# Own weight buffers, freer load order and shifted side work around the Wo product of an attention and mixer block

## Chip, cores, metric

The kernel runs on one core of one Trainium2 chip. The metric is the device time of one execution in microseconds (us), as the median of several runs. Times inside an execution ("at 1091 us") are from the start of its profiled span.

## The reference, cut to what matters

```python
x = A_x                                            # 2048 tokens of 1024, bf16
# sa, ca, ga, sb, cb, gb: six vectors made from silu(c) @ w_mod
h = layernorm(x) * (1 + ca) + sa
x = x + ga * A(h)        # 32 heads of 128, memory of 8 tokens; ends in o @ Wo (4096 -> 1024)
h = layernorm(x) * (1 + cb) + sb
x = x + gb * B(h)

def B(x):                                          # mixer
    h  = gelu(layernorm(x) @ w1)                   # 1024 -> 1024
    hs = shift_quarters(h) @ w2                    # quarters moved by 1, -1, 2, -2 tokens
    x1 = x + hs
    return x1 + gelu(layernorm(x1) @ w3) @ w4      # 1024 -> 3584 -> 1024
```

## The kernel before

The engines are TensorE (PE, the matmuls), VectorE (DVE), ScalarE (ACT) and GpSimd (POOL); SyncE (SP) here issues DMA transfers. ACT and POOL issue some too, each from its own queue. PE's sums go to PSUM, here 8 banks; the program uses a bank again only when another engine has emptied it (at 1491 us PE waits 6.79 us for that). A pool with `bufs=n` hands out n buffers in turn. PE is to be busy all the time. After the attention its stages are: the Wo product (32 units of 32 matmuls); A, the product with w1 and its gelu; the w2 product; then twice (for two "pairs" of 1024 tokens) w3 and w4, each made of seven Strassen-like products of half-size blocks, which need sums of blocks of z (the second layer norm, transposed by DMA). Their weights come in by "ring" loads. A "snap" is a bank that ACT copies to SBUF, a "join" is DVE's sum of a bank and a snap (in w4: a scaled bank), and an "addend" (rs) is what POOL prepares to be added to an output of w4.

The Wo stage. `keep_order` pins an instruction: pinned instructions of one queue keep the order in which the code emits them. An unpinned one may be put wherever its dependencies allow by the scheduler that builds the program.

```python
otpA = ...tile_pool(name="x1_otA", bufs=3)         # + otpB, bufs=3, opened later
wspR = ...tile_pool(name="x1_wsR", bufs=1)
ws_pools[:] = [wsp, wsp, wspR]                     # wsp has 2: three Wo buffers in all
def load_ot(j):                                    # one head chunk of O, transposed
    ot = pool.tile([P, 8, 512], BF16, name="OTc")
    keep_order(nc.sync.dma_start(ot[:], OTx_d[j // 4, j % 4]))
def W_units(blk):                                  # blk: 512 tokens
    def f():                                       # one unit: column half n2, head chunk hc
        if hc == 0: st["accs"] = [acc_tile() for _ in range(4)]
        woc = ws_tile([P, 8, 512])
        keep_order(nc.sync.dma_start(woc[:], Wo2[...]))
        ...  # 32 matmuls with ot, woc; after hc 3 the gate ga is applied
        if n2 == 1: load_ot(blk * 4 + hc + 6)      # refill when both halves have used it
    return [mk(n2, hc) for n2 in range(2) for hc in range(4)]
```

The w2 stage and the outputs of w4:

```python
def Ba(t):   # one tile of 128 tokens: load u (sync queue), 16 matmuls, x1b = acc + u,
    ...      # store x1b (ACT queue), layer norm -> z on ACT
def Bb(t):   # z -> z2a (tiles 0 to 7) or z2b (8 to 15)
    return lambda: nc.scalar.dma_start_transpose(z2s[t // 8][...], zs[t][:])
# after tile 11: z_sums(0), four DVE sums S1..S4 for the first pair

def fin(a, n, i, bank, s=None):                    # w4: one 128 x 512 output
    if s is not None: ...                          # two POOL operations on rs
    t_ = stm.tile(...)                             # stm: 3 buffers
    nc.vector.tensor_tensor(t_[:], st[i][bank][:], gbs_b[:, cs], ALU.mult)  # empties the bank
    o = outp.tile(...)
    nc.vector.tensor_tensor(o[:], t_[:], r[:], ALU.add)                     # waits for POOL
    nc.scalar.dma_start(out2[...], o[:])
# pair 0: z_sums(1), four sums in a row, before the sixth product of w4
```

## Time and profile before

| what | before |
|---|---|
| time, median of 3 | 1678.64 us (1678.47 to 1680.76) |
| span of the profiled run | 1680.5 us, mean granted clock 0.959 |
| Wo stage (first Wo product to first A product) | 321.3 us, of it 76.2 us waits for Wo loads |
| A | 55.6 us |
| w2 stage, to the third product on the sums of z | 90.5 us |
| from there to the first w4 product | 77.7 us |
| w4, w3, w4 after it | 94.3, 84.4, 84.8 us |

The stages are cut where the timeline of PE changes its line. The lines themselves are in the prediction.

### The profile page before, as it was taken

To read this page: it belongs to the slowest core of one execution; us is meant where nothing else is said; L and a number is where in the kernel's file an instruction comes from. 1 tells how busy PE (TensorE), PEld (TensorE's weight loads), DVE (VectorE), ACT (ScalarE), POOL (GpSimd) and SP (SyncE) were. 2 spreads that over 40 slices of the span, in tenths; PEclk is the share of its full clock that TensorE was granted. 3 is DMA by queue.
4 is the path that set the end of the run, shared out by engine and by line. 5 is a ranking of instruction groups with operands and counts; after the bars stand their busy time and mean duration, and the time that the engine had idled before them with its cause. 6 is when DMAs were issued, how large, how long until landed. Compare 5 with 4: busy or idle time off the path is not lost. (4 is left out here: it accounts for less than half of the span.)

```text
span 1680.5 us, 24001 instructions
## 1 busy us (share of the span) xinstructions
PE 1521.8 (91%) x9410; PEld 800.3 (48%) x9410; DVE 770.1 (46%) x1553; ACT 561.3 (33%) x1149; POOL 345.8 (21%) x468
## 2 busy tenths in 40 slices
PE   6899999999999999999957766869997799989998
PEld 3465565555555555555623322324443344434443
DVE  5516555565466354654420040505434534563454
ACT  2534444444444444444400020202332464016500
POOL 7310000000000000000011110211200256365525
PEclk9999999999999999999968888989999899999999
DMA  9589878979887776574396575759469878767862
GB/s 323 168 273 230 237 182 222 220 196 236 214 209 187 186 176 142 158 178 99 89 266 220 189 221 164 225 194 257 140 143 231 262 278 296 262 226 259 305 220 65
DMA packets 388333, 350.89 MB, mean 209 GB/s; under 512 B 203627, under 2 KB 331627, under 8 KB 381683
## 3 DMA queue, kind: packets, MB, share of 16 engines
q1 hardware_dynamic: 334256, 287.10, 60.5%
q10 hardware_dynamic: 46130, 34.90, 7.3%
q0 software_dynamic: 7824, 27.27, 5.1%
q8 instruction: 75, 1.23, 0.3%
q14 instruction: 48, 0.39, 0.1%
HBM read 221.27 MB, written 76.31 MB: 177 GB/s over the span
## 5 line engine op out<-in xcount | busy, mean ns | idle before, releaser
L751 PE MATMUL acc<-wstream,OTc 128*128 128x512 bf16 x1024 | 244.8, 404 | 76.2 <-DMA wstream<-in_A_Wo_dram 76.2
L317 PE MATMUL acc<-hh,wk 128*128 128x480 bf16 x1024 | 227.2, 367 | 1.3 <-DMA wk<-in_A_Wk_dram 1.3
L317 PE MATMUL acc<-hh,wv 128*128 128x480 bf16 x1024 | 227.9, 366 | 0.0
L317 PE MATMUL acc<-hh,wq 128*128 128x480 bf16 x1024 | 225.8, 370 | 0.6 <-DVE hh L425 0.5
L751 PEld LDWEIGHTS <-OTc 128*128 128x128 bf16 x1024 | 105.3, 103 | 215.5 <-issue 107.5
L664 POOL DMA_DIRECT2D OTx_d<-OT x32 | 24.3, 758 | 709.5 <-DMA OT<-O 556.1
L317 PEld LDWEIGHTS <-wq 128*128 128x128 bf16 x1024 | 97.7, 99 | 95.2 <-issue 3.5
L127 ACT ACTIVATE QT<-acc 128x480 bf16<-128x480 f32 (+1 forms) x192 | 87.9, 476 | 162.9 <-PE acc L317 157.6
L646 DVE TENSOR_TENSOR O<-ps_o,rin_all 99x384 bf16<-99x384 f32 (+2 forms) x256 | 133.3, 522 | 13.7 <-DMA MT<-O 6.7
L317 PEld LDWEIGHTS <-wk 128*128 128x128 bf16 x1024 | 95.9, 98 | 90.9 <-DMA wk<-in_A_Wk_dram 3.0
L125 ACT CAST KT<-acc 128x480 bf16<-128x480 f32 (+2 forms) x190 | 84.9, 464 | 151.5 <-PE acc L317 143.2
L125 ACT CAST VT<-acc 128x480 bf16<-128x480 f32 (+3 forms) x222 | 86.2, 420 | 147.5 <-PE acc L317 140.6
L317 PEld LDWEIGHTS <-wv 128*128 128x128 bf16 x1024 | 94.8, 97 | 81.5
L1049 PEld LDWEIGHTS <-ring 128*128 128x128 f16 (+1 forms) x784 | 77.5, 99 | 106.3 <-issue 16.4
L632 DVE TENSOR_TENSOR Em<-E,maskB 99x495 bf16<-99x495 bf16 (+1 forms) x128 | 48.4, 379 | 167.6 <-ACT E L630 167.3
L645 DVE RECIPROCAL rin_all<-ps_o 99x3 f32<-99x3 f32 (+2 forms) x256 | 44.1, 174 | 139.2 <-PE ps_o L643 139.1
L753 DVE TENSOR_TENSOR x<-acc,ga_b 128x512 f32<-128x512 f32 x32 | 21.7, 684 | 171.1 <-PE acc L751 167.4
L643 PE MATMUL ps_o<-V,Em 99*99 99x129 bf16 (+2 forms) x704 | 84.4, 225 | 17.1 <-DVE O L646 10.2
L643 PEld LDWEIGHTS <-Em 99*99 99x99 bf16 (+2 forms) x704 | 68.4, 128 | 49.0 <-DVE O L646 14.4
L1099 PEld LDWEIGHTS <-hq 128*128 128x128 bf16 (+1 forms) x560 | 55.3, 99 | 75.1 <-issue 10.0
L630 ACT ACTIVATE E<-ps_s 99x495 bf16<-99x495 f32 (+2 forms) x160 | 86.5, 542 | 2.8 <-DVE Em L632 2.3
L836 ACT ACTIVATE u<-x,ln_nmr,ln_rstd 128x1024 bf16<-128x1024 f32 x16 | 19.7, 1232 | 200.5 <-DVE ln_nmr L835 199.6
(188 smaller groups left out, 2038.5 us busy)
## 6 DMA issues: line engine op xcount, KB each, us to landing
wstream<-in_A_Wo_dram SPq DMA_DIRECT2D x34, 1024.0 KB, 9.6
OTx_d<-OT POOLq DMA_DIRECT2D x32, 512.0 KB, 6.8
OTc<-OTx_d SPq DMA_DIRECT2D x16, 1024.0 KB, 5.6
wstream<-in_B_w_dram SPq DMA_DIRECT2D x56, 256.0 KB, 6.3
ring<-w3t_d SPq DMA_DIRECT2D x14, 1024.0 KB, 8.2
ring<-w4t_d SPq DMA_DIRECT2D x8, 1792.0 KB, 7.2
ring<-w3b_d SPq DMA_DIRECT2D x14, 768.0 KB, 5.3
ring<-w4b_d SPq DMA_DIRECT2D x6, 1792.0 KB, 9.2
```

What stands on the lines that cost most here:

```text
L125: nc.scalar.copy(dst, src)
L127: nc.scalar.mul(dst, src, scale)
L317: nc.tensor.matmul(acc[:, 0:CH], lhsT=W[:, kt, hl * P:(hl + 1) * P], rhs=hh[:, kt, i * CH:(i + 1) * CH], start=(kt == 0), stop=(kt == KT - 1))
L630: nc.scalar.activation(E[:rows, 0:o], ps[:rows, 0:o], ACT.Exp)
L632: nc.vector.tensor_tensor(Em[:rows, c0:c0 + o], E[:rows, 0:o], mk[:rows, 0:o], ALU.mult)
L643: nc.tensor.matmul(ps[:rows, i, :], lhsT=Em[:k, col0(t):col0(t) + rows], rhs=V[:k, t, 0:DH + 1], start=True, stop=True)
L645: nc.vector.reciprocal(rin, ps[:rows, 0:n, DH])
L646: nc.vector.tensor_tensor(O[:rows, ts[0]:ts[0] + n, :], ps[:rows, 0:n, 0:DH], rin[:, :, None].to_broadcast([rows, n, DH]), ALU.mult)
L664: nc.gpsimd.dma_start(OTx_d[:, h // 8, :, h % 8, :].rearrange("b d t -> d b t"), flat.rearrange("p (b t) -> p b t", t=512))
L751: nc.tensor.matmul(accs[tt][:], lhsT=ot[:, hl, tt * P:(tt + 1) * P], rhs=woc[:, hl, :], start=(h == 0), stop=(h == H - 1))
L1049: nc.tensor.matmul(acc[:], lhsT=B[:, k, q * P:(q + 1) * P], rhs=A[:, k, :], start=(start and k == 0), stop=(k == 3), skip_group_check=True)
L1099: nc.tensor.matmul(acc[:], lhsT=L3[:, k, i * P:(i + 1) * P], rhs=R3[:, k, :], start=(start and k == 0), stop=(k == 13), skip_group_check=True)
```

## The change

Its intent: give the Wo stream its own buffers so that its loads run ahead; let both column halves of the first Wo block use the same early OTc tiles; take the transposes of the second layer norm from ACT, which also stores and normalizes; hold the last outputs of w4 back by two so that DVE empties PSUM banks first. Cut to its core (pool moves, the later place of the last memory product and the check's PSUM bank left out):

```diff
-        otpA = ...tile_pool(name="x1_otA", bufs=3, side="right")
-        wspR = ...tile_pool(name="x1_wsR", bufs=1, side="right")
-        ws_pools[:] = [wsp, wsp, wspR]
+        otcp = ...tile_pool(name="x1_ot", bufs=6, side="right")
+        wspR = ...tile_pool(name="x1_wsR", bufs=4, side="right")
+        ws_pools[:] = [wspR]
...
-            keep_order(nc.sync.dma_start(ot[:], OTx_d[j // 4, j % 4]))
+            nc.sync.dma_start(ot[:], OTx_d[j // 4, j % 4])
-                    keep_order(nc.sync.dma_start(woc[:], Wo2[...]))
+                    nc.sync.dma_start(woc[:], Wo2[...])
...   # block 0; 4 instead of 3 banks in psB, all 8 banks of PSUM in the rotation
+        for u in W0[1][0:3] + W0[0][3:] + W0[1][3:]:
+            u()
...
-            return lambda: nc.scalar.dma_start_transpose(z2s[t // 8][...], zs[t][:])
+            return lambda: nc.sync.dma_start_transpose(z2s[t // 8][...], zs[t][:])
-            if i == 11:
-                z_sums(0)
+            if i == 14:
+                for f in z_sums(0):
+                    keep_order(f())
...   # w4: stm 4 buffers; o and its store in end(), which lags
+                fins.append(end)
+                if len(fins) > 2 or s is None:
+                    fins.pop(0)()
-            if pair == 0:
-                z_sums(1)
+            zs1 = z_sums(1) if pair == 0 else []
             for i in prod("b", A22, 6, False):
                 fin(1, 0, i, "b")
+                for u in zs1[i:i + 1]:
+                    u()
+            for u in fins:
+                u()
```

More of the change, by code (lines that the diff above doesn't have):

```diff
@@ L220, in make_masks @@
             nc.gpsimd.tensor_copy(maskB[:].rearrange("p (t c) -> p t c", c=TW), mt[:, None, :].to_broadcast([P, 5, TW]))
+        wop = LM.enter_context(tc.tile_pool(name="up_wo", bufs=2))
+        otmp = LM.enter_context(tc.tile_pool(name="up_otm", bufs=2))
         LQ = ExitStack()
@@ L236, in first_pass @@
         rp = RX.enter_context(tc.tile_pool(name="x_rows", bufs=1, side="right"))
-        wsp = RX.enter_context(tc.tile_pool(name="x_ws", bufs=2, side="right"))
+        RW = ExitStack()
+        wsp = RW.enter_context(tc.tile_pool(name="x_ws", bufs=2, side="right"))
         ga_b = rp.tile([P, D], F32, name="ga_b")
@@ L506, in first_pass @@
             nc.gpsimd.memset(t[0:96, 0, :], 0.0)
-        wop = LA.enter_context(tc.tile_pool(name="up_wo", bufs=2))
         otp = LA.enter_context(tc.tile_pool(name="up_ot", bufs=2))
@@ L595, in prep_units, with M_units @@
             return units
-        def M_units(hp, use_psS=False):
+        def M_units(hp):
             def mk(g):
@@ L600, in f @@
                     wo2, OTm = state["wo2", hp], state["otm", hp]
-                    acc = psS.tile([P, 512], F32, name="ps_s") if use_psS else acc_tile()
+                    acc = acc_tile()
                     a3 = acc[:, 0:4 * NMEM].rearrange("p (k m) -> p k m", m=NMEM)
@@ L657, in keep @@
             if h % 2 == 0:
-                state["otm", h // 2] = otp.tile([P, 2, NMEM], BF16, name="OTm")
+                state["otm", h // 2] = otmp.tile([P, 2, NMEM], BF16, name="OTm")
             OTm = state["otm", h // 2]
@@ L714, in first_pass @@
         R0.close()
+        RW.close()
         RO = ExitStack()
-        otpA = RO.enter_context(tc.tile_pool(name="x1_otA", bufs=3, side="right"))
-        wspR = RO.enter_context(tc.tile_pool(name="x1_wsR", bufs=1, side="right"))
-        ws_pools[:] = [wsp, wsp, wspR]
-        ot_pools = [otpA]
+        otcp = RO.enter_context(tc.tile_pool(name="x1_ot", bufs=6, side="right"))
+        wspR = RO.enter_context(tc.tile_pool(name="x1_wsR", bufs=4, side="right"))
+        ws_pools[:] = [wspR]
         ots = {}
@@ L724, in load_ot @@
                 return
-            pool = ot_pools[0] if j % 6 < 3 else ot_pools[1]
-            ot = pool.tile([P, 8, 512], BF16, name="OTc")
-            keep_order(nc.sync.dma_start(ot[:], OTx_d[j // 4, j % 4]))
+            ot = otcp.tile([P, 8, 512], BF16, name="OTc")
+            nc.sync.dma_start(ot[:], OTx_d[j // 4, j % 4])
             ots[j] = ot
@@ L739, in f @@
                     if hc == 0:
-                        st["accs"] = [acc_tile() for _ in range(4)]
+                        st[n2] = [acc_tile() for _ in range(4)]
                     if hc == 3 and n2 == 0:
@@ L743, in f @@
                             x1s[blk * 4 + tt] = xpools["tp4"].tile([P, D], F32, name="x1")
-                    accs = st["accs"]
+                    accs = st[n2]
                     woc = ws_tile([P, 8, 512])
-                    keep_order(nc.sync.dma_start(woc[:], Wo2[hc * 1024:(hc + 1) * 1024, cs].rearrange("(h p) n -> p h n", p=P)))
+                    nc.sync.dma_start(woc[:], Wo2[hc * 1024:(hc + 1) * 1024, cs].rearrange("(h p) n -> p h n", p=P))
                     ot = ots[blk * 4 + hc]
@@ L755, in f @@
                         load_ot(blk * 4 + hc + 6)
-                    elif blk == 0 and hc == 3:
-                        load_ot(4)
-                        load_ot(5)
                 return f
-            return [mk(n2, hc) for n2 in range(2) for hc in range(4)]
+            return [[mk(n2, hc) for hc in range(4)] for n2 in range(2)]
         W0 = W_units(0)
@@ L765, in first_pass @@
         load_wo2(NHP - 2)
-        interleave(att[NHP - 1], M_units(NHP - 3) + [lambda: load_wo2(NHP - 1)] + M_units(NHP - 2) + W0[0:2])
-        for u in att["end"]:
-            u()
-        for u in W0[2:3] + M_units(NHP - 1, use_psS=True):
-            u()
-        W0 = W0[3:]
+        interleave(att[NHP - 1], M_units(NHP - 3) + [lambda: load_wo2(NHP - 1)] + M_units(NHP - 2) + W0[0][0:2])
+        for u in att["end"] + W0[0][2:3]:
+            u()
+        for j in range(3, 6):
+            load_ot(j)
         LA.close()
         LQ.close()
-        psB = PS.enter_context(tc.tile_pool(name="psB", bufs=3, space=PSUM))
-        pst = PS.enter_context(tc.tile_pool(name="pstX", bufs=1, space=PSUM))
-        acc_pools[:] = [psA, psB, psA, psA2, psA, psB, psB]
+        psB = PS.enter_context(tc.tile_pool(name="psB", bufs=4, space=PSUM))
+        acc_pools[:] = [psB]
         LZ = ExitStack()
@@ L787, in first_pass @@
         bsm = LT.enter_context(tc.tile_pool(name="x1_sm", bufs=8))
-        LO = ExitStack()
-        otpB = LO.enter_context(tc.tile_pool(name="x1_otB", bufs=3))
-        ot_pools.append(otpB)
-        load_ot(3)
+        for u in W0[1][0:3] + W0[0][3:] + W0[1][3:]:
+            u()
+        acc_pools[:] = [psA, psB, psA, psB, psA, psB, psA2, psB]
+        acc_ctr[0] = 0
+        for u in M_units(NHP - 1):
+            u()
         def check_a(kt):
@@ L803, in check_b @@
         def check_b():
-            pn = pst.tile([1, 512], F32, name="pn")
+            pn = acc_tile()[0:1, :]
             for kt in range(KT):
@@ L823, in check_b @@
             nc.vector.tensor_scalar(bad[:], okm[:], -1.0, 1.0, ALU.mult, ALU.add)
-            pb = pst.tile([1, 512], F32, name="pn")
+            pb = acc_tile()[0:1, :]
             nc.tensor.matmul(pb[:, 0:1], lhsT=ones_col[:], rhs=bad[:], start=True, stop=True)
@@ L865, in C1b @@
             return f
-        for u in W0:
-            u()
         for blk in range(1, 4):
             chain = lagged(C1a, C1b, list(range(4 * blk - 4, 4 * blk)), lag=1)
+            units = [u for us in W_units(blk) for u in us]
             if blk == 1:
@@ L877, in first_pass @@
                 nc.scalar.dma_start(Mc_d[:], Macc[:])
-            interleave(chain, W_units(blk))
-        LO.close()
+            interleave(chain, units)
         RO.close()
-        ws_pools[:] = [wsp]
         RH = ExitStack()
@@ L920, in dve @@
         def dve(dst, a, b, op):
-            nc.vector.tensor_tensor(dst, a, b, op)
+            return nc.vector.tensor_tensor(dst, a, b, op)
         ready = {}
@@ L954, in z_sums @@
             S1, S2, S3, S4 = (zs4[:, i] for i in range(4))
-            dve(S1, A21, A22, ALU.add)
-            dve(S2, S1, A11, ALU.subtract)
-            dve(S3, A11, A21, ALU.subtract)
-            dve(S4, A12, S2, ALU.subtract)
             zsum[pair] = (A11, A12, S4, A22, S1, S2, S3)
+            return [lambda: dve(S1, A21, A22, ALU.add), lambda: dve(S2, S1, A11, ALU.subtract),
+                    lambda: dve(S3, A11, A21, ALU.subtract), lambda: dve(S4, A12, S2, ALU.subtract)]
         LT2 = ExitStack()
@@ L984, in Bb @@
         def Bb(t):
-            return lambda: nc.scalar.dma_start_transpose(z2s[t // 8][:, :, t % 8 * P:(t % 8 + 1) * P], zs[t][:])
+            return lambda: nc.sync.dma_start_transpose(z2s[t // 8][:, :, t % 8 * P:(t % 8 + 1) * P], zs[t][:])
         for i, u in enumerate(lagged(Ba, Bb, list(range(NTT)), lag=1)):
@@ L1003, in first_pass @@
         st2 = RF.enter_context(tc.tile_pool(name="x3_s2", bufs=2, side="right"))
-        stm = RF.enter_context(tc.tile_pool(name="x3_sm", bufs=3, side="right"))
+        stm = RF.enter_context(tc.tile_pool(name="x3_sm", bufs=4, side="right"))
         rsq = RF.enter_context(tc.tile_pool(name="x3_rq", bufs=2, side="right"))
@@ L1108, in rs_load @@
                     nc.sync.dma_start(rs[a, n, i][:], rs_d[t * P:(t + 1) * P, n * 512:(n + 1) * 512])
+            fins = []
             def fin(a, n, i, bank, s=None):
@@ L1118, in fin, with end @@
                 nc.vector.tensor_tensor(t_[:], st[i][bank][:], gbs_b[:, cs], ALU.mult)
-                o = outp.tile([P, 512], BF16, name="o")
-                nc.vector.tensor_tensor(o[:], t_[:], r[:], ALU.add)
-                nc.scalar.dma_start(out2[t * P:(t + 1) * P, cs], o[:])
+                def end():
+                    o = outp.tile([P, 512], BF16, name="o")
+                    nc.vector.tensor_tensor(o[:], t_[:], r[:], ALU.add)
+                    nc.scalar.dma_start(out2[t * P:(t + 1) * P, cs], o[:])
+                fins.append(end)
+                if len(fins) > 2 or s is None:
+                    fins.pop(0)()
             def ed():
@@ L1157, in w4_stage @@
                 fin(1, 1, i, "b", "s5")
+            zs1 = z_sums(1) if pair == 0 else []
             for i in prod("b", A22, 6, False):
                 fin(1, 0, i, "b")
+                for u in zs1[i:i + 1]:
+                    u()
+            for u in fins:
+                u()
         with tc.manual_schedule():
```

## The prediction

> **What bounds the kernel now.** I read the page first, then the timeline of TensorE (PE) where its row of tenths dips, then the timelines of the queue or engine that each gap names. The page:
>
> ```profile
> PE   6899999999999999999957766869997799989998
> ...
> PEclk9999999999999999999968888989999899999999
> ...
> L751 PE MATMUL acc<-wstream,OTc 128*128 128x512 bf16 x1024 | 244.8, 404 | 76.2 <-DMA wstream<-in_A_Wo_dram 76.2
> ```
>
> Each slice is 42 us. PE is full in the first half (projections and attention), dips from slice 21 to 27 and twice later, and the granted clock dips with it. The row of line 751 is the Wo product: 32 units of 32 matmuls, each unit fed by one 1 MB load of Wo. All its idle time, 76.2 us, waits for those loads. The timeline of PE, then that of the SP DMA queue, over the same time:
>
> ```profile
> 866.12 23.19 PE L751 MATMUL acc<-wstream,OTc 128*128 128x512 bf16 x96 [1.11 <-DMA wstream<-in_A_Wo_dram]
> ...
> 918.39 8.85 PE L751 MATMUL acc<-wstream,OTc 128*128 128x512 bf16 x32 [8.23 <-DMA wstream<-in_A_Wo_dram]
> ...
> 1116.68 70.85 PE L751 MATMUL acc<-wstream,OTc 128*128 128x512 bf16 x320 [8.31 <-DMA wstream<-in_A_Wo_dram]
> 1187.37 31.24 PE L895 MATMUL acc<-zT,w1s 128*128 128x512 bf16 x144
> ```
>
> ```profile
> 910.19 0.33 SPq L727 DMA_DIRECT2D OTc<-OTx_d  x1
> 910.56 0.43 SPq L746 DMA_DIRECT2D wstream<-in_A_Wo_dram  x1
> 927.27 0.33 SPq L727 DMA_DIRECT2D OTc<-OTx_d  x1
> 927.69 1.00 SPq L746 DMA_DIRECT2D wstream<-in_A_Wo_dram  x2
> ```
>
> The pattern: a unit ends at 909.9, only then does the SP queue issue the next OTc load (its buffer was being read by that unit), and the Wo load stands behind it in the same in-order queue. It lands some 8 us later and PE starts at 918.4. The queue's own waits say the same: it waited 123.2 us, in 8 waits, at line 727 for the matmuls of line 751. Ten units end so. From 1116.68, where no OTc load is left to issue, ten units run without a gap at 7.09 us each. Elsewhere they run at the lower clock: 8.85 us for one after an 8 us gap.
>
> The two later dips. First the w2 stage, in the timeline of ACT's queue, then DVE, then PE:
>
> ```profile
> 1254.04 12.38 ACTq L985 DMA_TRANSPOSE z2a<-z  x1
> ```
>
> ```profile
> 1271.41 0.69 DVE L977 TENSOR_TENSOR x1b<-acc,u 128x512 f32<-128x512 f32 x1 [9.14 <-DMA x1b_d<-x1b]
> ...
> 1298.98 1.23 DVE L921 TENSOR_TENSOR zs<-z2a 128x2048 f16<-128x2048 bf16 x1 [7.93 <-DMA z2a<-z]
> ```
>
> ```profile
> 1300.93 8.72 PE L975 MATMUL acc<-w2s,h1T 128*128 128x512 bf16 x32 [8.26 <-DVE ln_ve L111]
> ...
> 1317.33 3.57 PE L1049 MATMUL bank_b<-z2a,ring 128*128 128x512 bf16 x8 [5.19 <-POOL ln_rstd L113]
> ```
>
> And PE near the end of the first w4 stage:
>
> ```profile
> 1490.98 9.27 PE L1099 MATMUL bank_b<-ring,hq 128*128 128x512 f16 x32 [6.79 <-DVE join L1118]
> ```
>
> In the w2 stage (1243 to 1317) ACT is held 12.4 us by issuing one transpose; the x1b stores behind it are late, DVE waits 9.1 us for an x1b buffer, then 7.9 us because the Strassen sums of z were put after tile 11, before their transposes have landed. DVE needs about 3.3 us a tile against PE's 3.45, so lost DVE time is never made up and surfaces as PE gaps. At 1491 PE waits for DVE to empty a bank; DVE had first waited for POOL at each output and then done four sums of z (2.2 us each) in a row.
>
> **What the Trainium skill says.** "Perfetto Trace Analysis", § Optimization Strategy: the same bubble repeating on the engine that should be full can mean too few buffers for the next tile. The trace agrees: 8 us gaps, with three Wo buffers and an OTc refill in front. "TensorE: Matmul & The Clock Gate", § What's actually happening: after an idle window of about 3.4 us the array falls to half clock and needs as long a busy window to return. The trace agrees: 8.85 us for a unit after a gap, 7.09 without. "DMA: Bandwidth & Descriptors", § Issuing engines are not separate DMA queues: all queues share the 16 engines, and another issuer saves only the issuer's time. So I count the transposes' move to SP as freeing ACT, not as bandwidth; the trace shows the DMA share at 1.01 over 1243 to 1328.
>
> **The change part by part.**
>
> *Wo stage.* PE's order as built is now straight: block 0 does column half 0 for head chunks 0 to 2, half 1 for 0 to 2, then the last chunk for both; all 8 PSUM banks serve. The SP order still has an OTc load before many Wo loads, but Wo has four buffers of its own and six OTc buffers. Counting through that order, the Wo load of unit n is now issued when unit n-4 ends, so three units, 21 us, lie between issue and need, against 9.6 us median landing. The wait at an OTc load no longer hurts. The x loads in the queue (they wait for POOL adds, up to 18 us) stand in places where the load behind them is needed 15 us or more later. Removed: 75.1 us of gaps after the first unit. Also removed: the clock loss. Stage now 1187.4 - 866.1 = 321.3. Stage after: first three units as now 23.0; 29 units at 7.09 = 205.6; the small memory products and check, 2; stalls from DMA crowding, 5 (my guess). Sum 235.6. Gain 86.
>
> Why 5 and not 0: block 1 must move 8 MB Wo, 4 MB OTc and 5 MB of the layer-norm chain in 8 x 7.09 = 57 us, 300 GB/s. The trace shows 321 GB/s over its first 40 us, so it fits, narrowly. In block 0 the loads waiting at 882 (3 OTc, 3 Wo) need about 6 MB / 340 GB/s = 18 us; I find the fifth unit's Wo landing within 2 us of when PE gets there.
>
> The start does not move: the first two Wo loads stand behind the same transposes in SP, issued at 858.9. The product that waited 5.9 us before it goes later, but PE then waits for Wo instead.
>
> *w2 stage.* ACT loses 16 transposes; SP gains them. x1b stores go out in time, the sums wait for tile 14. Now from 1243.0 to the first product on the sums at 1328.3: 85.3 us. After: 256 matmuls at 0.2165 = 55.4; the first two products 3.5; lag 8 (DVE's 3.3 x 16 + 4 x 1.2 for the sums = 57.6, so 2 to 3 behind, plus 5 for late loads of u, which now stand behind transposes in SP, and a saturated DMA). Sum 66.9. Gain 18.
>
> *w4, first pair.* Outputs lag two steps and the sums alternate with them, so a bank is emptied as soon as it is done. Gain 6.8 idle, plus about 2.3 for the half clock after it: 9.
>
> *End.* The last outputs are held back by two: two more 0.69 us operations after the last bank. Loss 1.5.
>
> Sum: 86 + 18 + 9 - 1.5 = 111.5; 1678.6 - 111.5 = 1567.
>
> **The rivals.**
> 1. DMA becomes the bound of the Wo stage. For: the share of DMA is already 0.67 over the stage with 27% of it idle PE; the same work in 236 us needs 0.67 x 321 / 236 = 0.91. Against: the attention part runs at 0.9 to 1.0 in some 40 us windows (480 to 520: 1.02) with PE full. If true, stalls of 25 us instead of 5: about 1587.
> 2. The w2 stage is bound by DMA already (share 1.01), so taking transposes from ACT only moves the wait to SP: late u loads take the place of late stores. Then 0 to 5 us gain there: 1582. In favour of my reading: at 1255 to 1263 that share goes with under 90 GB/s, so much of it is queueing, not work.
> 3. The head-of-line wait stays, since OTc loads still precede Wo loads in SP: then Wo gains half, about 1610. The count of buffers speaks against it.
> 4. Better than thought: no stalls, lag 3 instead of 8: 1557.
>
> **Range and chances.** 1567 with 80% from 1548 to 1592: the low end is rival 4 with the start somewhat earlier; the high end has rival 1 or 2 whole. A gain under 2% (over 1645) would need the Wo stage to gain under 50 us of its 99 idle or slow. Faster 0.97, same 0.02, slower 0.01.
>
> **What would show it.** Right: the Wo row's idle below 15 us with matmul mean near 380 ns; the clock at full from 875 to the end of A; the SP queue still waiting at the OTc line without PE noticing; Wo stage near 236 us; w2 stage to first sum product near 67; no PE gap over 2 us near the end of the first w4 stage. Wrong: gaps at Wo loads while DMA is at 1.0 (rival 1); DVE waiting for u loads in the w2 stage (rival 2); a new PE wait on a PSUM bank, since the check now takes banks of the shared rotation.

## The result, and the profile after

The changed kernel took 1566.58 us (median of 4, 1564.84 to 1573.46) against 1679.22 us of the kernel before in the same rounds: ratio 0.9336, 95% interval 0.9306 to 0.9365. The outputs are correct. The profiled run has a span of 1565.6 us at a mean clock of 0.981.

The page, and PE's timeline over the Wo stage:

```profile
PE   5799999999999999999996899999998899989998
...
PEclk9999999999999999999997899999999999999999
...
L753 PE MATMUL acc<-wstream,OTc 128*128 128x512 bf16 x1003 | 223.2, 383 | 7.8 <-DMA wstream<-in_A_Wo_dram 6.5
```

```profile
866.05 0.59 PE L753 MATMUL acc<-wstream,OTc 128*128 128x512 bf16 x1 [6.54 <-DMA wstream<-in_A_Wo_dram]
866.85 57.55 PE L753 MATMUL acc<-wstream,OTc 128*128 128x512 bf16 x249 [0.22 <-issue]
...
987.39 103.77 PE L753 MATMUL acc<-wstream,OTc 128*128 128x512 bf16 x471
1091.01 55.42 PE L891 MATMUL acc<-zT,w1s 128*128 128x512 bf16 x250
```

PE's dip in slices 21 to 27 has shrunk to slices 22 and 23, where the attention ends and the first Wo load is awaited; the clock's dip likewise. The 76.2 us of waits have become 7.8, of which 6.54 lie before the first product. (1003 of the 1024 matmuls are in the trace; a few per cent of the records are missing.)

| stage | before | after | gain | predicted gain |
|---|---|---|---|---|
| up to the first Wo product | 866.1 | 866.1 | 0.1 | 0 |
| Wo stage | 321.3 | 225.0 | 96.3 | 86 |
| A | 55.6 | 55.3 | 0.3 | 0 |
| w2 stage, to the third product on sums | 90.5 | 71.7 | 18.9 | 18, counted to the first such product (23.7 there) |
| to the first w4 product | 77.7 | 80.5 | -2.8 | 0 |
| w4, pair 0 | 94.3 | 84.8 | 9.5 | 9 |
| w3, pair 1 | 84.4 | 90.7 | -6.2 | 0 |
| w4, pair 1 | 84.8 | 84.8 | 0 | 0 |
| after the last matmul | 5.9 | 7.0 | -1.1 | -1.5 |
| sum | 1680.5 | 1565.6 | 114.9 | 111.5 |

Two gaps of PE stand at new places, one in front of the third product on the sums in the first w3 stage, one in front of the first such product in the second:

```profile
1217.91 3.57 PE L1044 MATMUL bank_b<-zs,ring 128*128 128x512 f16 x8 [6.48 <-ACT snap L1010]
...
1391.14 3.41 PE L1044 MATMUL bank_b<-zs,ring 128*128 128x512 f16 x8 [4.52 <-ACT snap L1010]
```

After each, the eight matmuls take 3.4 to 3.6 us instead of 1.89: the half clock again.

Only the second gap is new in substance. In the kernel before, DVE waited at the same first join for the same transposes, and PE had a gap two products earlier:

```profile
1330.99 1.29 DVE L1057 TENSOR_TENSOR join<-bank_e,snap 128x512 f32<-128x512 f32 x2 [8.42 <-DMA z2b<-z]
```

```profile
1328.25 3.54 PE L1049 MATMUL bank_b<-zs,ring 128*128 128x512 f16 x8 [5.32 <-ACT snap L1015]
```

So the 23.7 us gained up to the first product on the sums are in part a wait moved to the third; 18.9 us is the fairer count.

### The profile page after: what moved, and what is told of

It is laid out like the page before. It is cut to its first block, busy times and chain, and to the rows that moved or that the text cites. A ratio compares the mean times of both kernels' runs of the same rounds, so it can differ in the third digit from the quotient of the medians.

```text
span 1565.6 us, 23960 instructions
## 1 busy us (share of the span) xinstructions
PE 1492.3 (95%) x9347; PEld 794.9 (51%) x9410; DVE 763.2 (49%) x1553; ACT 561.1 (36%) x1149; POOL 343.9 (22%) x468
## 4 chain that ended last, share of the span: by engine, by line
PE 89%; DMA 5%; DVE 2%; SPq 1%; POOL 1%; issue 1%; ACT 1%; ACTq 0%; DVEq 0%; POOLq 0%
PE acc L321 37%; PE acc L753 14%; PE bank_b L1094 6%; PE bank_b L1044 6%; PE acc L331 4%; PE acc L891 4%; PE acc L969 3%; PE bank_d L1044 3%; PE ps_o L646 2%; PE bank_e L1094 2%; PE bank_d L1094 2%; PE ps_s L630 2%; PE bank_e L1044 1%; DMA V<-VT 1%; DMA wstream<-in_B_w_dram 1%
## 5 line engine op out<-in xcount | busy, mean ns | idle before, releaser
L753 PE MATMUL acc<-wstream,OTc 128*128 128x512 bf16 x1003 | 223.2, 383 | 7.8 <-DMA wstream<-in_A_Wo_dram 6.5
L321 PE MATMUL acc<-hh,wq 128*128 128x480 bf16 x1024 | 224.4, 369 | 0.9 <-DVE hh L429 0.5
L753 PEld LDWEIGHTS <-OTc 128*128 128x128 bf16 x1024 | 100.7, 99 | 129.2 <-issue 10.6
L633 ACT ACTIVATE E<-ps_s 99x495 bf16<-99x495 f32 (+2 forms) x160 | 86.5, 541 | 2.8 <-DVE Em L635 2.3
L1010 ACT COPY snap<-bank_b 128x512 f32<-128x512 f32 x72 | 40.5, 583 | 104.1 <-PE bank_b L1094 63.2
```

The lines of the kernel that those rows point to most:

```text
L321: nc.tensor.matmul(acc[:, 0:CH], lhsT=W[:, kt, hl * P:(hl + 1) * P], rhs=hh[:, kt, i * CH:(i + 1) * CH], start=(kt == 0), stop=(kt == KT - 1))
L633: nc.scalar.activation(E[:rows, 0:o], ps[:rows, 0:o], ACT.Exp)
L753: nc.tensor.matmul(accs[tt][:], lhsT=ot[:, hl, tt * P:(tt + 1) * P], rhs=woc[:, hl, :], start=(h == 0), stop=(h == H - 1))
```

## The experiments

Twelve kernels were run, all correct. In this table "against after" is the difference of the two ratios to the kernel before, times 1678 us, so that kernels of different rounds can be set side by side; the intervals are 0.2% to 0.35% (3 to 6 us) either way for each ratio, more for the difference of two.

| kernel | median us | ratio to before | against after | Wo stage us |
|---|---|---|---|---|
| after | 1566.58 | 0.9336 | | 225.0 |
| after, both loads pinned again | 1653.66 | 0.9858 | +88 | 310.6 |
| after, 3 Wo buffers | 1583.03 | 0.9432 | +16 | 238.6 |
| after, old column order | 1569.48 | 0.9349 | +2 | 224.3 |
| before, 4 Wo buffers | 1660.92 | 0.9889 | +93 | 304.2 |
| before, pins taken away | 1593.84 | 0.9490 | +26 | (*) |
| after, transposes on ACT | 1577.74 | 0.9399 | +11 | 225.9 |
| after, sums after tile 11 | 1570.06 | 0.9352 | +3 | 224.4 |
| after, old w4 outputs | 1570.01 | 0.9342 | +1 | 224.6 |
| after, small w3 buffers moved | 1577.65 | 0.9389 | +9 | 224.4 |
| after, outputs before the fourth sum | 1568.21 | 0.9333 | 0 | 224.3 |
| after, the last two together | 1575.26 | 0.9374 | +6 | 224.1 |
| that, addends earlier, stores on POOL | 1563.10 | 0.9326 | -2 | 223.6 |

(*) There the scheduler also moves Wo units into the attention, so the stage begins earlier, at 839.7; the first A product comes at 1099.4 us, 88 us before that of the kernel before (1187.4). w4 of pair 0 takes 98.7 us there against 94.3, which is why the whole kernel gains a little less.

### The Wo stage: which part of the change did it?

Three theories. A: the fourth Wo buffer, as the prediction has it. B: the pins, which the prediction does not name at all. C: both column halves of block 0 at once.

**Pins put back.**

```diff
-            nc.sync.dma_start(ot[:], OTx_d[j // 4, j % 4])
+            keep_order(nc.sync.dma_start(ot[:], OTx_d[j // 4, j % 4]))
-                    nc.sync.dma_start(woc[:], Wo2[...])
+                    keep_order(nc.sync.dma_start(woc[:], Wo2[...]))
```

> The changed kernel, but the OTc loads and the Wo loads are pinned to program order again, as they were before. Theory A (the fourth Wo buffer removed the Wo waits): the Wo stage stays near its 225 us and the time within 5 us of 1567. Theory B (the waits went because the scheduler is now free to put Wo loads ahead of OTc loads in the SP queue): gaps of some 8 us come back after OTc loads, the stage grows to 270 to 320 us and the time to 1610 to 1660 us. Theory C (opening both column halves of block 0 did it): no change, as A.

Measured: 1653.66 us, Wo stage 310.6 us. Almost the whole gain is gone, with four Wo buffers, six OTc buffers and the new column order all in place. PE, then the SP queue, in this kernel:

```profile
905.74 9.59 PE L753 MATMUL acc<-wstream,OTc 128*128 128x512 bf16 x31 [10.20 <-DMA wstream<-in_A_Wo_dram]
923.40 9.29 PE L753 MATMUL acc<-wstream,OTc 128*128 128x512 bf16 x32 [8.07 <-DMA wstream<-in_A_Wo_dram]
940.77 4.00 PE L753 MATMUL acc<-wstream,OTc 128*128 128x512 bf16 x9 [8.07 <-DMA wstream<-in_A_Wo_dram]
```

```profile
882.34 1.29 SPq L729 DMA_DIRECT2D OTc<-OTx_d  x3
...
895.57 0.33 SPq L729 DMA_DIRECT2D OTc<-OTx_d  x1
895.94 0.43 SPq L748 DMA_DIRECT2D wstream<-in_A_Wo_dram  x1
915.36 0.33 SPq L729 DMA_DIRECT2D OTc<-OTx_d  x1
915.73 0.43 SPq L748 DMA_DIRECT2D wstream<-in_A_Wo_dram  x1
```

And the SP queue of the changed kernel over the same time:

```profile
882.81 1.29 SPq L729 DMA_DIRECT2D OTc<-OTx_d  x3
884.20 8.54 SPq L748 DMA_DIRECT2D wstream<-in_A_Wo_dram  x3
...
896.80 0.35 SPq L729 DMA_DIRECT2D OTc<-OTx_d  x1
897.20 0.43 SPq L748 DMA_DIRECT2D wstream<-in_A_Wo_dram  x1
```

Count the Wo loads. Up to 882 us both kernels have issued four. The code emits the OTc refill at the end of a unit, ahead of the next unit's Wo load, and pinned loads keep that order. So at 895.57, when the fourth unit has ended and set the OTc buffer free, the pinned queue issues the refill and behind it the fifth Wo load: the one that PE needs now. It starts 10.20 us later. Without pins three Wo loads pass at 884.20 while their buffers are free, and the load behind the same refill at 897.20 is the eighth: three units lie between its issue and its use. The queue still waits for matmuls at the OTc line (35.0 us in 8 waits in the changed kernel, 120.5 us in 8 waits with the pins), but what stands behind that wait is no longer urgent.

**Three Wo buffers.** One number, `bufs=4` to `bufs=3`.

> The changed kernel with 3 instead of 4 Wo buffers, the number there was before. Theory A (the fourth buffer): with one unit of look-ahead fewer, the load behind an OTc load is issued about 7 us later and lands late: gaps of 3 to 8 us at several of the ten OTc loads, the stage 250 to 300 us, the time 1590 to 1640 us. Theory B (the scheduler's freedom) and theory C (both column halves): the time within 10 us of 1567.

Measured: 1583.03 us, stage 238.6 us, the Wo row's idle time 19.5 us. The fourth buffer is worth some 16 us once the order is free, 13.6 of them in this stage. That lies between what theory A (1590 to 1640) and theory B (within 10 of 1567) expected: the buffer matters, but it is not what made the gain.

**Old column order in block 0.**

```diff
-        for u in W0[1][0:3] + W0[0][3:] + W0[1][3:]:
+        for u in W0[0][3:] + W0[1]:
```

> The changed kernel with the old order of the first Wo block: column half 0 for all four head chunks, then half 1. Theory C (both halves open at once spare the wait at block 0, because the early OTc tiles serve two units each while the late ones are still on their way): the fourth unit needs the late fourth OTc tile at once, a gap of 5 to 15 us in block 0 and the time 1572 to 1582 us; with C as the whole cause 1600 or more. Theory A: no more than 5 us of difference, since the six OTc buffers and four Wo buffers are there.

Measured: 1569.48 us, stage 224.3 us, without a gap in block 0. The order of the columns is not worth anything that these runs can show.

**Four buffers in the kernel before.**

```diff
-        wspR = ...tile_pool(name="x1_wsR", bufs=1, side="right")
+        wspR = ...tile_pool(name="x1_wsR", bufs=2, side="right")
-        ws_pools[:] = [wsp, wsp, wspR]
+        ws_pools[:] = [wsp, wspR]
```

> The kernel before with 4 instead of 3 Wo buffers and nothing else changed. Theory A (the fourth buffer is enough by itself): the Wo stage falls from 321 us to 230 to 260 us, the time to 1590 to 1620 us. Theory B (program order holds the loads back, whatever the buffers): the gaps behind the OTc loads stay at 8 us, the stage 300 to 321 us and the time 1660 to 1680 us. Theory C: as B.

Measured: 1660.92 us against 1677.97, stage 304.2 us. Gaps of 8 us stay (8.15 and 8.08 at 915 and 933 us), as theory B expected. Buffers behind a closed door help little.

**Pins taken from the kernel before.** The reverse of the first edit, nothing else.

> The kernel before with only the two pins taken away (OTc and Wo loads free of program order); three Wo buffers, the split OTc pools and the old column order stay. Theory B as the last runs left it (the pins made the wait, the fourth buffer is worth the 16 us by which the kernel with three was slower): the Wo stage falls from 321 us to 235 to 255 us, the time to 1592 to 1615 us. If pins and the fourth buffer work only together: the stage stays above 290 us and the time above 1645 us.

Measured: 1593.84 us against 1678.41. With three buffers, the old pools and the old column order, taking two `keep_order` away gives 85 of the 112 us. The stage falls to 259.7 us, short of the 235 to 255 expected, because it begins 26 us earlier. This settles it for theory B.

### The w2 stage: the transposes, or the place of the sums?

**Transposes back on ACT.**

```diff
-            return lambda: nc.sync.dma_start_transpose(z2s[t // 8][...], zs[t][:])
+            return lambda: nc.scalar.dma_start_transpose(z2s[t // 8][...], zs[t][:])
```

> The changed kernel with the transposes of the second layer norm issued by ACT again. Theory D (the issue on ACT made the stores late and DVE wait): the way from the first w2 product to the first product on the sums grows from 61.6 us to 75 to 85 us, ACT shows transposes of over 8 us again, and the time is 1580 to 1592 us. Rival E (the place of the four sums, after tile 14 and not 11, made the gain): within 5 us of 1567.

Measured: 1577.74 us, 11 us over the changed kernel, short of the 13 to 25 expected. To the first product on the sums it is 79.2 us, to the third 86.5. ACT is held again, and DVE waits for the stores behind:

```profile
1158.11 8.73 ACTq L979 DMA_TRANSPOSE z2a<-z  x1
```

```profile
1172.30 0.69 DVE L971 TENSOR_TENSOR x1b<-acc,u 128x512 f32<-128x512 f32 x1 [5.96 <-DMA x1b_d<-x1b]
```

Here PE runs all 256 matmuls of w2 without a gap (55.4 us) and the lag shows up whole behind them, as gaps of 10.51 and 7.20 us. In the kernel before, and in the one with four buffers, the same lag made gaps inside the stage. A likely reason is the eighth PSUM bank in the rotation, which lets PE run further ahead of DVE; no run tested that alone.

**Sums after tile 11 again.** One number, `i == 14` to `i == 11`.

> The changed kernel with the four sums of z put after tile 11 again. Theory D: the transposes have nearly landed by then, so DVE waits at most 3 us at the first sum and the time stays within 4 us of 1567. Rival E: DVE waits some 8 us at the first sum, as before, PE gets gaps of 4 to 8 us late in the w2 stage, and the time is 1575 to 1587 us.

Measured: 1570.06 us. To the third product on the sums it is 77.2 us. Kernels whose w2 code is that of the changed kernel have 71.7 to 75.9 us there (the changed kernel, and those with pins, three buffers, old columns and old w4 outputs), so the place of the sums is worth between 1 and 6 us, which these runs cannot tell from their own spread; theory D's time (within 4 us of 1567) holds, and DVE does not wait at the first sum at all (7.93 us in the kernel before, where ACT issued the transposes). The move of the transposes is the main part: by the same count, 86.5 us against 71.7 to 75.9, it is worth 11 to 15 of the 18.9 us.

### The two new gaps

**Old w4 outputs.** The lag of two, the fourth join buffer and the spread sums undone.

> The changed kernel with the outputs of w4 as they were: no lag of two, three join buffers, the sums of the second pair in a row before the sixth product. Theory F (the lag took some 9.5 us from the first w4 stage and gave some 6 back at the start of the next w3 stage, where ACT stands behind stores of held-back outputs): w4 of pair 0 grows from 84.8 to 94 us, the w3 stage after it falls from 90.7 to 84.5 us, the end is 1 us shorter, and the time is 1568 to 1571 us. Rival (the loss at the start of that w3 stage is not from the lag): it stays near 90 us and the time is 1575 to 1577 us.

Measured: 1570.01 us. w4 of pair 0 is 94.4 us (84.8 in the changed kernel), the w3 stage after it 84.4 us (90.7): the lag gains 9.6 us and gives 6.2 back. The trade is shown; the total, 3 us in medians, is inside the noise.

Why it gives them back: ACT issues the stores of the held-back outputs in its own order and stands there until DVE has made them. ACT, then DVE, in the changed kernel:

```profile
1359.16 31.24 ACTq L1121 DMA_DIRECT2D out_dram<-o  x11
1390.50 1.07 ACT L1010 COPY snap<-bank_b 128x512 f32<-128x512 f32 x2 [30.83 <-DMA out_dram<-o]
```

```profile
1384.41 2.29 DVE L917 TENSOR_TENSOR zs<-z2b,zs 128x2048 f16<-128x2048 bf16 x1
1386.62 3.41 DVE L1120 TENSOR_TENSOR o<-join,rs 128x512 bf16<-128x512 f32 x2
```

**Outputs before the fourth sum.**

```diff
             for i in prod("b", A22, 6, False):
                 fin(1, 0, i, "b")
+                while i == 3 and fins:
+                    fins.pop(0)()
                 for u in zs1[i:i + 1]:
                     u()
-            for u in fins:
-                u()
```

> The changed kernel with the two held-back outputs of the first w4 stage finished before the fourth sum instead of after it. Theory F: ACT's stores go out about 2 us after the last bank, the 4.5 us gap at the start of the next w3 stage and the half clock after it go, that stage falls from 90.7 to 84.5 to 87 us, the time 1561 to 1564 us. Rival (ACT is late because of the number of stores, not of their wait): the gap stays above 3 us.

Measured: 1568.21 us, and the gap is still 3.69 us; the w3 stage is 90.0 us. A miss for theory F. The gap is in the range that the rival (the number of stores) named, but ACT still waits for DVE: its snap comes at 1388.88, right after the last output (1388.41). The outputs come before the fourth sum now, but three of them take 5.01 us instead of 3 times 0.69:

```profile
1383.40 5.01 DVE L1120 TENSOR_TENSOR o<-join,rs 128x512 bf16<-128x512 f32 x3
```

At that time POOL works on the first addends of the next stage (from 1380.2 to 1387.9), while a join that reads a PSUM bank keeps its 0.69 us. The Trainium skill says, "SBUF — State Buffer", § SBUF: two separate sides, that a DVE operation with two SBUF inputs and a GpSimd operation that reads SBUF exclude each other for a whole instruction. This trace agrees: 1.67 us an output with POOL at work; the last run below has 0.63 us without.

**Small w3 buffers moved.** In the changed kernel the first join of the first w3 stage waits for a transpose of z: DVE waits 5.36 us, ACT's gelu waits for the join, and the snap that PE needs stands behind the gelu. That the join buffers lie where the z tiles of w2 were is inferred from this wait. The edit opens the large hq and ring pools last, so that they, not the joins, lie there:

```diff
-        hq_p = ...tile_pool(name="x3_h", bufs=1, side="right")
-        ring_pools[1] = ...tile_pool(name="x3_rB", bufs=2, side="right")
         stA = ...   # and st2, stm, rsq, gsp
+        hq_p = ...tile_pool(name="x3_h", bufs=1, side="right")
+        ring_pools[1] = ...tile_pool(name="x3_rB", bufs=2, side="right")
```

> The changed kernel with the small buffers of the w3 stage (snaps, joins, addends) placed where the w2 operands lay, and the large hq and ring buffers where the last z tiles lie. Theory G (the 6.5 us gap at the third product on the sums comes because the join buffers share memory with z tiles that wait for their transposes): DVE no longer waits for a transpose at the first join, the gap falls to under 2 us, the half clock after it goes, first w2 product to third product 60 to 65 us instead of 71.7, the time 1557 to 1562 us. Rival (the gap comes from DVE or ACT being late by itself): the gap stays above 4 us and the time within 3 us of 1567.

Measured: 1577.65 us, slower than the changed kernel. The gap itself went as expected (0.16 us before the third product; it comes 68.8 us after the first w2 product, not in 60 to 65), and the first w4 product came at 1291.2 us instead of 1298.4. Then w4 took 96.0 us instead of 84.8:

```profile
1336.52 0.61 PE L1094 MATMUL bank_e<-ring,hq 128*128 128x512 bf16 x1 [8.87 <-DVE hq L917]
```

```profile
1322.08 1.74 DVE L1120 TENSOR_TENSOR o<-join,rs 128x512 bf16<-128x512 f32 x1 [8.81 <-DMA rs<-rs_d]
```

The outputs of w4 need addends (rs) that POOL makes during w3. Their first load now stands in the SP queue behind a ring load that waits for the last z tiles. POOL begins them at 1225.3 us instead of 1218.2 and ends them at 1311.6 instead of 1304.2. PE was 7 us earlier and the addends 7 us later, and the slack between them was less than 14. So theory G holds for the gap and misses the time.

**Both edits.**

> Both of the two edits before in one kernel. If the two gaps are independent the gains add: 1551 to 1557 us, faster than the changed kernel by 10 to 15 us.

Measured: 1575.26 us, a miss, with the same stall in w4 (8.33 us). The gains do not add, because neither edit gains on its own.

**Addends earlier, stores on POOL.** On top of both:

```diff
+            if pair == 0:
+                for u in add[0:2]:
+                    u()
+                add = add[2:] + [lambda: None] * 2
             for g in range(7):
...
-                    nc.scalar.dma_start(out2[...], o[:])
+                    (nc.gpsimd if pair == 0 and s is None else nc.scalar).dma_start(out2[...], o[:])
```

> The kernel with both edits, and two more: the addends of the first w3 stage start one group earlier (two of them before the first product), and the last outputs of the first w4 stage are stored from the POOL queue instead of ACT's. Theory H (with the buffers moved, the w3 stage ends 7 us sooner than the chain of addends on POOL, whose first load stood behind ring loads that now wait for the z transposes; so the first w4 outputs came late and PE waited 8.9 us in w4): that gap falls under 2 us, w4 of pair 0 is back at 84 to 86 us, and with ACT free of stores the gap at the start of the next w3 stage falls under 2 us: 1552 to 1560 us, faster than the changed kernel by 7 to 15 us. Rival (what is gained at one gap always comes back at the next, because POOL and DVE have too little slack): 1563 to 1577 us.

Measured: 1563.10 us (1560.96 to 1569.45), ratio 0.9326, interval 0.9301 to 0.9350. w4 of pair 0 is back at 84.8 us, so theory H holds for the stall. The second gap is gone: w3 of pair 1 takes 84.4 us. The two new edits ran together; which one did what is read from the trace. POOL, whose queue now waits with the stores, starts its next addend only at 1386.5 us, after the last output (1385.7), and the outputs are fast:

```profile
1383.77 1.89 DVE L1124 TENSOR_TENSOR o<-join,rs 128x512 bf16<-128x512 f32 x3
```

But the first gap is back (4.75 us) by another way: the addends that were moved forward stand in POOL's queue before the last small layer-norm operation of w2, and DVE, then ACT, then PE wait for it.

```profile
1218.08 0.16 DVE L834 SCALAR_TENSOR_TENSOR ln_nmr<-ln_mv,ln_rstd 128x1 f32<-128x1 f32 x1 [6.19 <-POOL ln_rstd L113]
```

It beats the kernel before. That it beats the changed kernel is not shown, since their intervals overlap. The obvious next step, that small operation ahead of the addends, was not tried.

## Why the prediction was right or wrong, point by point

The time, 1566.58 against 1567, is right. The reasons are right in part, and that the time is met to within 1 us is luck.

- **What bounds the kernel.** Right: the gaps at the Wo loads were the largest loss, and the head of the SP queue made them. Experiments with the pins show the same queue with and without the gaps. Three readings were inexact: "ten units end so" (ten gaps from 918 on, but eight of 7.4 to 9.5 us and two near 3, as the 8 waits say), 27% idle PE (76.2 of 321.3 us is 24%) and 909.9 (the unit ends at 910.2).
- **"Wo has four buffers of its own ... the Wo load of unit n is now issued when unit n-4 ends."** The observation is right, the count of the order as built agrees with the trace. The cause read into it is wrong. The step that failed is that the four buffers put the load early and so remove the wait: with them and the pins the gaps stay (310.6 us), and without pins three buffers already give most of the gain. The pins were in the diff and the prediction passed over them. The buffers are worth some 16 us of it.
- **Rival 3, "the count of buffers speaks against it".** The rival (a half-kept wait, 1610) did not happen, but what spoke against it was the free order, not the count.
- **Wo stage, 235.6.** Measured 225.0, so the stage was put 10 us too long. The 5 us for DMA crowding did not occur: the DMA share was 1.05 to 1.08 in the windows from 920 to 1040 us and PE lost nothing. And a unit takes 6.91 us (103.62 us for the last 15), not 7.09, a figure which held the half clock after the gap ahead of it: 29 times 0.18 is the other 5.
- **Rival 1** (DMA bound): did not happen.
- **w2 stage, gain 18.** 23.7 to the first product on the sums, 18.9 to the third. The mechanism, stores freed on ACT, is shown by the run with the transposes put back. The lag at the first product was 2.7 us (61.6 - 55.4 - 3.5) instead of 8, and the wait at the first join was overlooked. Rival 2 (late u loads in the SP queue) shows only as 2.4 us of DVE's waiting in 3 waits, so at most 2.7 us of PE.
- **w4, gain 9.** Measured 9.5. The old outputs put back show it (9.6). Missed: that ACT would stand at the stores of the held-back outputs and give back 6 us at the start of the next w3 stage. The prediction asked what a late output does to the PSUM bank, not who waits for the output.
- **End, loss 1.5.** Measured 1.1.
- **In sum** the gain of the Wo term was 10 us too small, w2 (to the first product on the sums) and w4 together 6 too small, and 14 us lost in the two w3 stages were not foreseen (7.7 from that product to the first w4 product, 6.2 in the second). These partly cancel, which is why the total agrees better than its terms.

## What to carry to other kernels

When an engine waits for loads that stand behind another wait in an in-order queue, first ask which load is at the head, and what holds the order; here two pins outweighed the buffers five to one. Look for pins and emission order in a diff as carefully as for sizes. And a gap closed near the end of a chain is worth only the slack of whatever chain comes second: before closing it, find that chain (here the addends on POOL) and start it earlier, or the time comes back one stage later.

## What the Trainium skill lacked or had wrong

- "Perfetto Trace Analysis", § Optimization Strategy, gives too few buffers as what a repeating bubble can mean. Here the same bubble, eight gaps of 7.4 to 9.5 us, came from the order of loads in one in-order queue: a buffer more took 17 us away (1677.97 to 1660.92), a free order 85 us (1678.41 to 1593.84). The section could name this second cause and how to tell it apart: count which load stands behind the queue's wait.
- "DMA: Bandwidth & Descriptors", § Issuing engines are not separate DMA queues, calls the sequencer time that another issuer saves usually small relative to the DMA itself. The median agrees (1.67 us for an issue of the sixteen z transposes in the kernel before, with 9.8 and 3.9 us to landing for z2a and z2b), but together they held ACT for 43.6 us, one of them for 12.38 us, and moving them took 11 us from the whole kernel. The section does not say that work behind a long issue in the same queue waits.
- No page that was read gives the cost, at this shape, of a DVE operation that meets a busy POOL; the runs show 1.67 us against 0.63 us for a 128 x 512 output with two f32 inputs in SBUF, in agreement with the lock that "SBUF — State Buffer" describes.
